# Crossbar transposes for two more units of a chunk-selected attention with a gated FFN, row copies as transfers, and an instruction order drawn anew

## The chip, the cores and the metric

One core of a Trainium2 chip runs the whole program. The metric is the time of one execution on the device in microseconds; a version's time is the median of its runs. Five engines work side by side, each through its own queue in program order: TensorE (PE, with the weight load PEld beside it), VectorE (DVE), ScalarE (ACT), GpSimd (POOL) and SyncE (SP), which here issues transfers and computes nothing.

## What is computed

The inputs q, k and v have 4 batches, 8 heads, 768 rows and 64 columns. For every query row, 6 of the 24 chunks of 32 keys are chosen by an upper bound on the score; the scores of the chosen keys at or before the row go through a softmax and weigh v. The result, 3072 rows of 512, goes through a gated feed-forward layer.

```python
k_min, k_max = k_chunks.min(axis=3), k_chunks.max(axis=3)      # 24 chunks of 32 rows
ub = sum(maximum(q * k_min, q * k_max))                        # bound for every row and chunk
ub = where(row // 32 >= chunk, ub, -1e9)
top_chunks = argsort(ub)[..., -6:]
scores = where(chosen & (row >= column), q @ k.T / 8, -1e9)
attn_out = softmax(scores) @ v
x = attn_out as 3072 x 512
out = (sigmoid(x @ w_gate) * (x @ w_val)) @ w_out              # 512 -> 1536 -> 512
```

## The kernel before

The 24 blocks of 128 rows (4 batches of 6) are put into eight units of up to three blocks. Unit 0 holds the first blocks of batches 0, 1 and 2; unit 1 three blocks of batch 0; unit 2 the last two blocks of batch 0 and, as a third, the first block of batch 3; units 3 to 7 hold the rest of batches 1, 2 and 3. The first block of a batch needs no choice of chunks and goes through a helper of its own, `first()`.

What a unit goes through:

- **Keys and queries.** They come in by `load_first`, `load_wide` (units 1 and 2) or `load_blocks` (batches 1 to 3: four transfers of 384 KB each for `k` and for `q`, named `k00_3` to `k11_3` and so on), and are turned so that the head's columns lie on partitions. `first()` and `turned()` turn on TensorE against an identity; `keys_blocks()` and `turn_queries()` turn on VectorE. The turned keys are copied by rows into `hk` (`hk0_*` and `hk1_*`, 64 partitions each), the queries into `hq`, the chunks' minima and ranges into `kcr` (`kx0`, `kx1`).
- **The choice.** `choose()` computes the bounds on TensorE (`ub`), takes the sixth largest per row on VectorE, and writes the mask, turned back, into the other 64 partitions of `hq` (the copies `hqm0_*`, `hqm1_*`), so that the score product adds it.
- **Attention.** `attend()`: score banks on TensorE (`sc`), the exponential on ScalarE (`exp`), the triangle on GpSimd (`cm`), the product with v (`pv`), and in `finish()` the division on VectorE (`rz`, `x`).
- **The turn of the result.** The attention rows `x` are turned into `xT` for the feed-forward layer. In `finish()` units below `XBAR` do it with `xps` (one TensorE transpose for each block) and a copy `xT` out of PSUM on ACT or DVE; units from `XBAR` on with one crossbar transpose on SP (`xT`, L905). `XBAR` is 4.
- **The feed-forward layer.** Units 0 to 3 each have their own: 12 pairs of `g` and `v` (four matmuls of 384 columns each), a tanh on ACT, `hg` on DVE, then `o0`, `o1`, `o2` (four matmuls of 512 columns each) for each of three blocks. Units 4 and 5, and 6 and 7, go through it as pairs, with seven products for eight (`ffn_pair`): products P1 to P7, sums of weights `Sg`, `Sv` and `So`, sums of activations `T` on DVE, copies `E` and additions `C` on ACT and DVE, `hg`, then sums S1 to S4 on POOL or DVE and the projection Q1 to Q7.

No loop sets the order of the instructions. `Plan.add` records every operation with its reads, writes, candidate engines and costs; a string `ORDER` in the file names all operations in one line of text, with the engine (`@POOL`) and the buffer slots (`:0,3`) of each, and `Plan.order()` emits them in that order, each into its engine's queue. The order was drawn by a planner that is not in the file; the costs, the transfers' times (`dma=`) and a mark `port=True` for operations that it is to keep from meeting on a shared port are what it is given. Buffers come in numbered slots, so a transfer into a slot waits for the last reader of what was there: `k_3` takes the slot of `k_2`, `q_3` that of `q_2`, the `v` blocks take six.

SP's queue holds the loads, the stores and the crossbar transposes. GpSimd's queue holds the loads of the three weights.

Of the kernel before, what the change touches and what calls it, by code (L numbers as in the profile page):

```python
# [15 lines left out]
XBAR = 4  # L16
# [103 lines left out]
g_u0_11:1,0,11 kx1_u2_3 cm_u1_0 sc_u1_0_1:4 kt_u2_3@DVE:0 v_u0_11:7 hkf1 exp_u1_0_1 kx0_u2_3 tanh_u0_9 v16_0_3  # L120
o0_u0_0:4,0 kt_u2_0:2 hg_u0_9 tanh_u0_11 hk1_u2_3@POOL hk1_u2_0 kt_u2_1:1 sc_u1_1_1:5 q2_u2 o1_u0_0 hg_u0_11
hk0_u2_1@ACT q3_u2 kx0_u2_1 exp_u1_1_1 k11_1:0 hq1_u1_0 qf1_3:2 v16_0_2 o2_u0_0 v16_0_1 hk0_u2_3@POOL pv_u1_2:6
osb_u0_0@DVE kfT_3:3 qn_u2_3:4 sc_u1_5_0:2,2 kcr_u2 qn_u2_2:2 pv_u1_1:1 kf16_3@DVE:0 qf0_3 pv_u1_0 qT_u2_3:7 out_u0_0
rz_u1_0:0 qT_u2_2:0 sc_u1_6_2:5,3 pv_u1_3 k01_1 qf_u2_2 sc_u1_7_0:4,0 exp_u1_5_0 rz_u1_1:1 o0_u0_1:3,1 vf_3:1 qm_u2_2
qf_u2_3@DVE hq0_u2_2 x_u1_0:0 exp_u1_6_2 sc_u1_7_2:0 sc_u1_4_2:2,1 x_u1_1:2 exp_u1_7_2 sc_u1_7_1:7 o1_u0_1 exp_u1_4_2
qm_u2_3 exp_u1_7_0 qm_u2_0 sc_u1_5_2:1 hq1_u2_1 sc_u1_6_0:5 cm_u1_7 exp_u1_7_1 sc_u1_5_1:0 cm_u1_5 exp_u1_5_1
sc_u1_4_0:6 ub_u2:2,4 k10_1 exp_u1_6_0 k00_1 exp_u1_5_2 xps_u1_0:7,1 exp_u1_4_0 sc_u1_6_1:0 ubn0_u2:0 sc_u1_4_1:5
qfT_3:1 xT_u1_0 exp_u1_4_1 cm_u1_4 mx0_u2:0 o2_u0_1 hk0_u2_0@ACT hq0_u2_3@POOL ubn1_u2 exp_u1_6_1 hq1_u2_3@POOL
pv_u1_5:2 qf16_3:6 mx1_u2 cm_u1_6 pv_u1_7:6 vc_3@ACT pv_u1_4 v_0_5:5 hq1_u2_0@DVE pv_u1_6 rz_u1_2:0 scf_3:7,5,0 ap1_u2
# [15 lines left out]
g_u1_10:2,3,3 tanh_u1_9 qf0_u3_3 v_u1_10:0 v_1_4:1 tanh_u1_10 hg_u1_9 qm_u3_2@POOL exp_u2_5_0 sc_u2_5_2:4
g_u1_11:5,0,5 hg_u1_10 hk1_1_0@ACT x_u2_0:1 v_u1_11:2 hg_u1_8 cm_u2_5 hq0_u3_2@ACT ub_u3:3,6 cm_u2_4 v_2_1:5
hq0_u3_0@POOL tanh_u1_11 v_1_2:3 hk1_1_3@ACT hg_u1_11 v16_1_0 o0_u1_0:0,1 ubn1_u3:0 hq1_u3_0@ACT hk0_1_1 qf0_u4_2
k01_2 xps_u2_0:7 o1_u1_0 ubn0_u3 hk0_1_0 hk0_1_3@ACT ubm1_u3 mx1_u3:0 o2_u1_0 exp_u2_5_2 ubm0_u3 ap1_u3 xT_u2_0@ACT
hq1_u3_2 o0_u1_1:1,0 osb_u1_0 qf0_u4_3 mx0_u3 sc_u2_5_1:5 out_u1_0 o1_u1_1 exp_u2_5_1 ap0_u3 hk0_1_2@ACT apt1_u3:0
q10_2:1 pv_u2_5:2 apt0_u3 pv_u2_6:6 q00_2 pv_u2_4 hqm1_u3_2@ACT hqm0_u3_0@DVE hqm0_u3_2 o2_u1_1 kx1_2_2:1 hk1_1_2  # L150
sc_u3_0_0:3,3 sc_u3_0_1:4 xps_u2_1:7 exp_u3_0_0 sc_u3_0_2:0 sc_u3_1_0:5,1 rz_u2_2:0 hqm1_u3_0 pv_u2_7 x_u2_2:2
osb_u1_1 o0_u1_2:3,1 kx1_2_1 q11_2 xT_u2_1@ACT cm_u3_0 exp_u3_0_1 sc_u3_1_1:2 exp_u3_1_0 rz_u2_3:0 kx0_2_1
sc_u3_3_0:1,0 exp_u3_0_2 sc_u3_6_1:7,2 o1_u1_2 cm_u3_1 exp_u3_1_1 x_u2_3:1 k16_2_3@ACT:5 v16_1_2 kx0_2_0 sc_u3_1_2:4
out_u1_1 k16_2_0:4 exp_u3_1_2 sc_u3_3_2:5 o2_u1_2 k16_2_1@ACT:1 kx1_2_0 xps_u2_3:0 xps_u2_2:4 xT_u2_2 xT_u2_3@ACT
# [10 lines left out]
hq1_u4_0@POOL cm_u3_5 v16_2_2 hq1_u4_2@POOL v_1_5:0 v16_1_5 cm_u3_4 hg_u2_6 mx0_u4 ap0_u4 apt0_u4:0 hqm0_u4_2
qf0_u5_1:1 tanh_u2_8 g_u2_9:3,2,13 v_u2_9:4 g_u2_10:1,3,14 tanh_u2_9 hg_u2_7 hg_u2_9 exp_u3_7_2 exp_u3_5_1 sc_u3_4_1:6
hqm0_u4_0@DVE pv_u3_6:2 tanh_u2_10 hg_u2_8 v_u2_10:7 hg_u2_10 g_u2_11:4,2,15 v_u2_11:0 exp_u3_4_1 sc_u4_2_0:7,2
sc_u4_2_3:6 exp_u4_2_3 hk0_2_1 v_2_0:2 hk1_2_1 k01_3 k00_3 k16_3_0:4 kx0_3_0 k16_3_3:0 exp_u4_2_0 cm_u4_2 v16_1_4
pv_u3_5:1 xps_u3_0:3 sc_u4_2_1:5 exp_u4_2_1 tanh_u2_11 pv_u3_7 rz_u3_3:0 x_u3_3:2 o0_u2_0:6,1 sc_u4_3_2:5,3 exp_u4_3_2
pv_u3_4 sc_u4_0_2:4,1 sc_u4_0_3:2 exp_u4_0_3 sc_u4_3_0:7 exp_u4_3_0 hg_u2_11 o1_u2_0 o2_u2_0 osb_u2_0 sc_u4_1_0:7,0  # L170
sc_u4_3_1:2 v_3_2:0 sc_u4_3_3:5 exp_u4_3_3 xT_u3_0 qf0_u6_0 qf0_u5_3 ap1_u4 qf0_u5_2 rz_u3_2:0 sc_u4_2_2:3 hk1_2_3
qf0_u5_0 cm_u4_3 v16_2_0 exp_u4_1_0 cm_u4_1 o0_u2_1:0,0 o1_u2_1 kx1_3_3:1 hk1_2_0 hq0_u5_2@POOL hq1_u5_2@POOL
qm_u5_2@ACT:0 sc_u4_1_1:7 exp_u4_3_1 qm_u5_0@ACT exp_u4_0_2 x_u3_2:1 sc_u4_1_3:1 o2_u2_1 exp_u4_1_3 kx0_3_3 kt_3_0:3
apt1_u4 kx0_3_1 kt_3_3:4 hqm1_u4_0 xps_u3_3:2 osb_u2_1 q11_3:1 k16_3_1:5 q10_3 out_u2_0 xps_u3_2:5 xT_u3_2@ACT
o0_u2_2:6,1 kx1_3_2 ub_u5:0,1 ubn1_u5:0 ubn0_u5 mx0_u5:0 kx1_3_0 ap0_u5 kt_3_1:0 sc_u4_1_2:5 hqm1_u4_2@ACT sc_u4_0_0:4
exp_u4_0_0 hq1_u5_0@POOL hq0_u5_0@POOL xT_u3_3@ACT o1_u2_2 o2_u2_2 g_u3_0:2,2,0 v_u3_0:4 exp_u4_2_2 pv_u4_2:3
# [1188 lines left out]
```

## Time and profile before

| | |
|---|---|
| median of 3 runs | 288.0 us (287.28 to 288.57) |
| the profiled execution | 286.49 us, of which the span from the first to the last instruction 284.5 us |
| mean granted TensorE clock | 0.998 |
| instructions | PE 2668, DVE 660, ACT 457, POOL 231 |
| moved by the transfers | 34.28 MB, mean 120 GB/s |
| crossbar transposes | 16, all on SP's queue |

The profile shows one execution. A busy time is a sum over an engine's instructions; a strip of 40 digits gives the busy share in tenths of 40 equal slices of the span (7.1 us each). Matmuls overlap: a single one of 384 columns shows 326 ns, while four in a row take 0.65 us, so a duration that is to be added up is read from start to start. The last 2 us of the execution's time (286.49 less 284.5) lie outside the span.

### The profile page before, as it was taken

What the parts mean: (1) busy time and instruction counts of PE and PEld (TensorE: products, weight loads), DVE (VectorE), ACT (ScalarE), POOL (GpSimd) and SP (SyncE); (2) the same over time, 40 slices, a digit from 0 to 9 for tenths busy, and PEclk for the clock granted to TensorE, in tenths of its full rate; (3) what the DMA queues carried; (4) which work ended last, traced back from release to release, by engine and by line L of the source; (5) the groups of instructions that cost most, each with busy time, mean ns of one, the idle gap of its engine ahead of it and who ended that gap; (6) DMA issues with size and microseconds to landing.
All of it is one profiled execution on the core that took longest, in us unless ns stands there. A gap on an engine that the chain in (4) does not pass through costs nothing.

```text
span 284.5 us, 7266 instructions
## 1 busy us (share of the span) xinstructions
PE 265.6 (93%) x2668; PEld 180.9 (64%) x2668; DVE 248.8 (87%) x660; ACT 209.5 (74%) x457; POOL 162.1 (57%) x231
## 2 busy tenths in 40 slices
PE   1859999799999999999999999999899999999994
PEld 1637565567764666664767756676476786765784
DVE  6569987569998998989979899999999989999972
ACT  2477579488779788668799997899899647758621
POOL 7298634246257559569776866357848700076720
PEclk9999999999999999999999999999999999999999
DMA  7999999999999999919335013030000211001005
GB/s 169 254 214 219 213 197 206 197 186 221 186 181 215 188 247 210 175 30 216 80 75 140 6 30 81 37 69 13 16 14 17 64 40 75 2 37 76 1 2 221
DMA packets 130035, 34.28 MB, mean 120 GB/s; under 512 B 118096, under 2 KB 127056, under 8 KB 130000
## 3 DMA queue, kind: packets, MB, share of 16 engines
q1 hardware_dynamic: 125248, 29.11, 48.5%
q0 software_dynamic: 4752, 4.72, 9.9%
q8 instruction: 21, 0.34, 0.5%
q14 instruction: 14, 0.11, 0.1%
HBM read 30.67 MB, written 6.29 MB: 130 GB/s over the span
## 4 chain that ended last, share of the span: by engine, by line
PE 66%; DVE 11%; DMA 9%; SPq 4%; ACT 3%; POOL 3%; issue 2%; DVEq 0%; POOLq 0%; ACTq 0%
PE sc_u L848 9%; PE o_u L968 9%; PE g_u L937 8%; PE v_u L937 8%; PE pv_u L881 5%; DMA kq_u<-in_k_dram 5%; DMA v<-in_v_dram 4%; PE suo_u6u L1195 3%; PE suo_u4u L1195 2%; PE ube_u L787 2%; PE suv_u6u L1054 2%; DVE hg_u L1084 2%; PE sug_u6u L1054 2%; DVE hgp_u L1084 2%; SPq L538 2%
## 5 line engine op out<-in xcount | busy, mean ns | idle before, releaser
L859 ACT ACTIVATE att_u<-sc_u 128x512 f16<-128x512 f32 (+3 forms) x184 | 92.1, 552 | 15.9 <-PE sc_u L848 14.4
L865 POOL TENSOR_SCALAR_AFFINE_SELECT att_u<-att_u 128x384 f16<-128x384 f16 (+1 forms) x56 | 30.7, 556 | 44.3 <-ACT att_u L859 35.5
L937 PE MATMUL g_u<-xT_u,wg 128*128 128x384 f16 x192 | 39.1, 326 | 0.1
L937 PE MATMUL v_u<-xT_u,wv 128*128 128x384 f16 x192 | 39.0, 326 | 0.1
L968 PE MATMUL o_u<-wo,hg_u 128*128 128x512 f16 x144 | 35.3, 379 | 1.0 <-DMA wo<-in_moe_w_out_dram 1.0
L949 DVE SCALAR_TENSOR_TENSOR hg_u<-gate_u,v_u 128x384 f16<-128x384 f16 x48 | 25.1, 535 | 4.3 <-PE v_u L937 2.4
L881 PEld LDWEIGHTS <-att_u 128*128 128x128 f16 x640 | 24.9, 98 | 5.5 <-issue 1.5
L881 PE MATMUL pv_u<-v,att_u 128*128 128x65 f16 x640 | 27.3, 193 | 1.1 <-POOL v L564 1.0
L945 ACT ACTIVATE gate_u<-g_u 128x384 f16<-128x384 f32 x48 | 23.3, 495 | 6.7 <-PE g_u L937 6.5
L848 PE MATMUL sc_u<-hqe,hke 128*128 128x128 f16 (+2 forms) x220 | 27.8, 243 | 0.1
L848 PE MATMUL sc_u<-hqo,hko 128*128 128x128 f16 (+2 forms) x220 | 27.3, 243 | 0.1
L937 PEld LDWEIGHTS <-wg 128*128 128x128 f16 x192 | 18.1, 98 | 10.4 <-issue 0.8
L937 PEld LDWEIGHTS <-wv 128*128 128x128 f16 x192 | 18.1, 98 | 10.5 <-DMA wv<-in_moe_w_val_dram 0.4
L968 PEld LDWEIGHTS <-hg_u 128*128 128x128 f16 x144 | 13.2, 98 | 13.7 <-DVE kcr L572 1.3
L848 PEld LDWEIGHTS <-hke 128*128 128x128 f16 x220 | 17.0, 98 | 7.3 <-issue 1.0
L848 PEld LDWEIGHTS <-hko 128*128 128x128 f16 x220 | 16.8, 98 | 6.4 <-issue 0.9
L1177 POOL TENSOR_TENSOR v<-v,hg_u 128x384 f16<-128x384 f16 x6 | 6.0, 996 | 24.1 <-PE sug_u6u L1054 22.3
L564 POOL CAST v<-v 128x512 f16<-128x512 f32 x23 | 14.8, 644 | 7.0 <-DMA v<-in_v_dram 5.8
L900 DVE TENSOR_TENSOR x_u<-pv_u,rz_u 128x384 f16<-128x384 f32 (+1 forms) x28 | 14.7, 529 | 0.6
L1054 PEld LDWEIGHTS <-Sg 128*128 128x128 f16 x96 | 9.1, 98 | 6.1 <-issue 1.4
L810 DVE MAX8 mx_u<-ubn_u 128x8 f32<-128x8 f32 (+16 forms) x152 | 12.5, 158 | 0.3
L1054 PEld LDWEIGHTS <-Sv 128*128 128x128 f16 x96 | 9.0, 98 | 5.4 <-issue 0.5
(280 smaller groups left out, 699.3 us busy)
## 6 DMA issues: line engine op xcount, KB each, us to landing
v<-in_v_dram SPq DMA_DIRECT2D x23, 256.0 KB, 4.1
k<-in_k_dram SPq DMA_DIRECT2D x12, 384.0 KB, 5.0
q<-in_q_dram SPq DMA_DIRECT2D x12, 384.0 KB, 5.0
out_dram<-osb_u SPq DMA_DIRECT2D x16, 256.0 KB, 2.6
wg<-in_moe_w_gate_dram POOLq DMA_DIRECT2D x3, 512.0 KB, 11.5
wv<-in_moe_w_val_dram POOLq DMA_DIRECT2D x3, 512.0 KB, 12.8
wo<-in_moe_w_out_dram POOLq DMA_DIRECT2D x3, 512.0 KB, 20.3
out_dram<-osb_u6u SPq DMA_DIRECT2D x5, 256.0 KB, 2.4
```

The lines of the kernel that those rows point to most:

```text
L564: plan.add(f"v16_{b}_{ib}", {POOL: pool(H * D)}, lambda e: nc.gpsimd.tensor_copy(v16[b % 2][:, ib, :, 0:D], at(t)), reads=[t], writes=[("v ...
L848: nc.tensor.matmul(at(t)[:, o:o + 128 * m], hk[b % 2][e_][:, p, 128 * jb:128 * jb + 128], hq[u.side][e_][:, p, 128 * x:128 * (x + m)], sta ...
L859: plan.add(f"exp_{u.name}_{h}_{y}", {ACT: act(n)}, lambda e, t=t, att=att, b0=b0, n=n: nc.scalar.activation(at(att)[:, b0:b0 + n], at(t), ...
L865: nc.gpsimd.affine_select(out=dv, in_=dv, compare_op=ALU.is_ge, fill=0.0, base=0, pattern=[[0, u.m], [1, 128]], channel_multiplier=-1)
L881: nc.tensor.matmul(at(pv)[:, last, x, :], at(att)[:, c:c + 128], v16[b % 2][:, jb, h, :], start=(jb == 0), stop=(jb == ib))
L900: plan.add(f"x_{u.name}_{p}", {DVE: dve(u.t)}, lambda e: nc.vector.tensor_tensor(at(x_).rearrange("p a (e d) -> p e a d", e=2), at(pv)[:, ...
L937: nc.tensor.matmul(at(t), w16[:, c, 128 * fb:128 * fb + 128], at(u.xt)[:, c, :], start=(c == 0), stop=(c == 3))
L945: plan.add(f"tanh_{u.name}_{fb}", {ACT: act(T)}, lambda e, g=g, gate=gate: nc.scalar.activation(at(gate), at(g), AF.Tanh, scale=0.5), read ...
L949: plan.add(f"hg_{u.name}_{fb}", {DVE: dve(T)}, lambda e, w_=w_, gate=gate, hg=hg: nc.vector.scalar_tensor_tensor(at(hg), at(gate), 1.0, at ...
L968: nc.tensor.matmul(at(o), hgs[c][1][1]()[:, 128 * tb:128 * tb + 128], wo16[:, fc, lo:hi], start=(c == 0), stop=(c == NFB - 1))
L1054: nc.tensor.matmul(at(t), left[i](c), right[i](c), start=first and c == 0, stop=c == 1, skip_group_check=not first)
L1195: nc.tensor.matmul(at(t), sums[what[i][0], f][1]()[:, 128 * tb:128 * tb + 128], what[i][1](f), start=first and f == 0, stop=f == half - 1, ...
```

## The change

`XBAR` goes from 4 to 2: units 2 and 3 turn their attention rows by crossbar transposes too (4 transfers each in place of 8 and 12 TensorE transposes and 8 copies out of PSUM). In `first()`, the fourth batch's block, which belongs to unit 2, does the same with its queries, keys and result: two casts to 16 bits (`qfc_3` on POOL, `kfc_3` on ACT) and two crossbar transposes take the place of eight 32-bit TensorE transposes and two copies out of PSUM, and two crossbar transposes that of four TensorE transposes and two copies. The row copies `hk` of batches 2 and 3 and `hqm` of units 4 to 7 may be plain transfers on SP; in the new order 12 of the former and 9 of the latter are. `hg` of the pairs gets the mark `port=True` unless one source is PSUM. The order is drawn anew: it is the same up to about 40 us and another after that. Crossbar transposes go from 16 to 28, and SP issues 33 transfers more in all.

The code, without the string of the order:

```diff
-XBAR = 4
+XBAR = 2
...
@@ -353,6 +353,8 @@
             nc.scalar.copy(o, i)
         elif e == DVE:
             nc.vector.tensor_copy(o, i)
+        elif e == SP:
+            nc.sync.dma_start(o, i)
         else:
             nc.gpsimd.tensor_copy(o, i)
 
@@ -593,6 +595,14 @@
         cols = slice(128 * x, 128 * x + 128)
         half = {}
         for n in "kq":
+            if u.i >= XBAR:
+                flat = Buf("np", f"{n}fc_{b}", [128, H * D], F16)
+                plan.add(f"{n}fc_{b}", {POOL: pool(H * D), DVE: dve(H * D, 2), ACT: act(H * D, False)}, lambda e, n=n, flat=flat: copy(
+                    e, at(flat), at(raw[n]).rearrange("s h d -> s (h d)")), reads=[(raw[n], 0), (raw[n], 1)], writes=[flat], port=True, prio=next_())
+                half[n] = Buf("np", f"{n}f16_{b}", [128, NP, 128], F16)
+                plan.add(f"{n}f16_{b}", {SP: (60, 60)}, lambda e, h=half[n], flat=flat: nc.sync.dma_start_transpose(out=at(h), in_=at(flat)),
+                         reads=[flat], writes=[half[n]], prio=next_(), dma=(1200, 256))
+                continue
             t = ps(f"{n}fT_{b}", "pr", [128, NP, 128])
 
             def turn(e, t=t, n=n):
@@ -659,6 +669,12 @@
             plan.add(f"xf_{b}_{e_}", {DVE: dve(256)}, lambda e, pv=pv, rz=rz, x_=x_: nc.vector.tensor_tensor(
                 at(x_), at(pv)[:, :, 0:D], at(rz).unsqueeze(2).to_broadcast([128, NP, D]), ALU.mult),
                 reads=[pv, rz], writes=[x_], prio=next_())
+            if u.i >= XBAR:
+                op = plan.add(f"xTf_{b}_{e_}", {SP: (60, 60)}, lambda e, x_=x_, e_=e_: nc.sync.dma_start_transpose(
+                    out=at(u.xt)[:, 2 * e_:2 * e_ + 2, cols], in_=at(x_).rearrange("s p d -> s (p d)")),
+                    reads=[x_], writes=[(u.xt, c, x) for c in (2 * e_, 2 * e_ + 1)], prio=next_(), dma=(1200, 256))
+                plan.hold(op, u.xt) if u.xt not in op.bufs else None
+                continue
             t = ps(f"xpsf_{b}_{e_}", "pr", [128, 2, 128], F16)
 
             def turn(e, t=t, x_=x_):
@@ -738,7 +754,7 @@
             plan.add(f"kt_{b}_{p}", {DVE: dve(S)}, lambda e, k16=k16, kt=kt: nc.vector.transpose(
                 at(kt), at(k16).rearrange("p c d -> p (c d)")), reads=[k16], writes=[kt], prio=next_())
             for e_ in range(2):
-                plan.add(f"hk{e_}_{b}_{p}", {POOL: pool(S), DVE: dve(S, 4, 64), ACT: act(S, False, 64)},
+                plan.add(f"hk{e_}_{b}_{p}", {POOL: pool(S), DVE: dve(S, 4, 64), ACT: act(S, False, 64), **({SP: (60, 60)} if b > 1 else {})},
                          lambda e, p=p, e_=e_, kt=kt: copy(e, hk[par][e_][ROWS[e_], p], at(kt)[ROWS[e_]]),
                          reads=[kt], writes=[("hk", par, jb, e_, p) for jb in blocks], port=True, prio=next_())
         ranges(par, f"{b}", kx, slice(0, NC), blocks, next_)
@@ -822,7 +838,8 @@
                 at(apt)[:, e_], ap[u.side][:, e_, 0:u.nb].rearrange("p c d -> p (c d)")),
                 reads=[("ap", u.side, e_)], writes=[(apt, e_)], prio=next_())
             for p in range(0, NP, 2):
-                plan.add(f"hqm{e_}_{u.name}_{p}", {POOL: pool(2 * u.n), DVE: dve(2 * u.n, 4, 64), ACT: act(2 * u.n, False, 64)},
+                plan.add(f"hqm{e_}_{u.name}_{p}", {POOL: pool(2 * u.n), DVE: dve(2 * u.n, 4, 64), ACT: act(2 * u.n, False, 64),
+                                                   **({SP: (60, 60)} if u.i > 3 else {})},
                          lambda e, p=p, e_=e_: copy(
                              e, hq[u.side][e_][MASK[e_], p:p + 2, u.s0:u.t],
                              at(apt)[32 * p:32 * p + 64, e_, :].unsqueeze(1).to_broadcast([64, 2, u.n])),
@@ -1083,7 +1100,7 @@
                         plan.add(f"hg_{tag}_{x}_{fb}", {DVE: dve(T)},
                                  lambda e, src=src, g=g, o=o: nc.vector.scalar_tensor_tensor(
                                      o(), at(g), 1.0, at(src), ALU.add, ALU.mult), reads=[g, src], writes=[okey],
-                                 prio=next_(EV))
+                                 port=c != 2, prio=next_(EV))
 
                 op = mul(1, u_, True)
                 for b in (q_, r_):
```

Of the order, one place that the prediction speaks of: the loads of batch 3's keys and the crossbar transposes of unit 3 on SP. Between these words stand those of other engines.

```
... k01_3 v_3_5 hk0_2_1@SP out_u1_0 k10_3 xT_u3_1 k00_3 k11_3 v_2_4 hk1_2_0@SP v_2_0 xT_u3_0 xT_u3_3 xT_u3_2 ... g_u3_0 ...
```

More of the change, by code (lines that the diff above doesn't have):

```diff
@@ L120 @@
[L120 to L129, printed above, removed]
@@ L145 @@
[L145 to L154, printed above, removed]
@@ L165 @@
[L165 to L174, printed above, removed]
@@ new lines @@
+g_u0_10:4,3,10 tanh_u0_10 v_u0_10:6 kT_u2_3:7 hq1_u1_1@POOL hq1_u1_0@POOL v16_0_3 cm_u1_3 hk0_u2_0 g_u0_11:4,1,11
+v_u0_11:2 tanh_u0_11 hg_u0_11 kx0_u2_2 hq0_u2_0@POOL hk1_u2_1@POOL sc_u1_0_1:0 o0_u0_0:4,0 o1_u0_0 hg_u0_9 hg_u0_10
+o2_u0_0 exp_u1_0_1 kx1_u2_3 v16_0_2 qm_u2_0@POOL osb_u0_0 kx0_u2_1 kx1_u2_2 kx1_u2_1 kx0_u2_3 k01_1 o0_u0_1:1,1
+o1_u0_1 v16_0_1 pv_u1_2:4 sc_u1_6_1:5,2 hk1_u2_2@ACT kt_u2_3@DVE:0 hqm1_u1_0@DVE hk0_u2_3@ACT sc_u1_6_2:7 cm_u1_0
+pv_u1_0:6 exp_u1_6_1 exp_u1_6_2 pv_u1_1 rz_u1_0:0 x_u1_0:1 k11_1 sc_u1_7_1:3,3 k00_1 sc_u1_5_0:5,1 exp_u1_5_0 pv_u1_3
@@ new lines @@
+xT_u3_3 ap1_u4 qf0_u6_0 qf0_u6_1 apt1_u4 hqm1_u4_0 pv_u3_5 rz_u3_2:0 x_u3_2:1 xT_u3_2 kx1_3_2:1 exp_u4_3_1 ub_u5:0,6
+ubn0_u5:0 hqm1_u4_2@ACT sc_u4_1_0:4,1 exp_u4_1_0 sc_u4_1_2:1 exp_u4_1_2 exp_u4_3_3 sc_u4_2_0:7 exp_u4_2_0
+hq1_u5_0@POOL o1_u2_1 o2_u2_1 q01_3:1 q10_3 cm_u4_3 hk0_2_0 k16_3_1:1 sc_u4_2_2:7 exp_u4_2_2 q00_3 osb_u2_1 out_u2_1
+kx1_3_0 kx0_3_2 kx0_3_0 kx0_3_1 sc_u4_4_2:2,3 exp_u4_4_2 exp_u4_2_1 mx0_u5:0 hq0_u5_0@ACT sc_u4_4_1:1 v16_2_0
+exp_u4_4_1 o0_u2_2:4,1 o1_u2_2 o2_u2_2 g_u3_0:5,2,4 cm_u4_2 v_u3_0:2 tanh_u3_0 g_u3_1:1,3,8 k16_3_3@ACT:6 v_u3_1:5
```

290 lines of the change are left out of this document (155 added, 135 removed).

## The prediction

> **What bounds the kernel now.** I read the page's engine totals and strips first, to see which engine is full where.
>
> ```profile
> PE 265.6 (93%) x2668; PEld 180.9 (64%) x2668; DVE 248.8 (87%) x660; ACT 209.5 (74%) x457; POOL 162.1 (57%) x231
> ...
> PE   1859999799999999999999999999899999999994
> ...
> DVE  6569987569998998989979899999999989999972
> ...
> DMA  7999999999999999919335013030000211001005
> ```
>
> TensorE is the fullest engine and has holes only at the start, around slice 7, and at the end. The transfers fill their engines up to slice 17 (121 us), which is where most of the new transfers go. VectorE is at nine tenths nearly everywhere. Next the busy times by stage, cut at 60, 120, 176 (just ahead of the first product of the pair of units 4 and 5) and 268 (where the last projections begin).
>
> ```profile
> 30.00:60.00 30.00, 27.71 (x270) 17.36 (x269) 21.65 (x81) 20.87 (x52) 11.51 (x23) 1.00 1.11 200
> 60.00:120.00 60.00, 59.90 (x644) 39.29 (x643) 56.53 (x170) 49.05 (x104) 36.50 (x58) 1.00 1.09 202
> 120.00:176.00 56.00, 56.00 (x717) 37.76 (x715) 52.02 (x166) 45.61 (x94) 42.85 (x56) 1.00 0.41 85
> 176.00:268.00 92.00, 89.63 (x796) 60.73 (x794) 88.27 (x177) 73.83 (x172) 45.98 (x55) 1.00 0.12 37
> ```
>
> The first column after the stretch is its length, then PE, PEld, DVE, ACT and POOL busy; the last three are the granted clock, the transfers' share and GB/s. From 60 to 176 us TensorE idles 0.1 of 116 us: each matmul taken out there is time, and each late transfer too. From 176 to 268 TensorE idles 2.4 us and VectorE 3.7: two bounds side by side. Last, what TensorE waited for.
>
> ```profile
> PE qfT L600 <- POOL hke L357: 5.8, 1, 5.8
> ...
> PE pv_u L881 <- POOL v L564: 1.0, 1, 1.0
> PE o_u L968 <- DMA wo<-in_moe_w_out_dram: 1.0, 1, 1.0
> ```
>
> The 5.8 us is the start. The two waits of 1.0 us stand at 50 and 52 us, behind 40 us, from where the order is new.
>
> **The change part by part.** *The turns leave TensorE.* Two places of the timeline show what one costs from start to start.
>
> ```profile
> 52.51 0.63 PE L600 MATMUL kfT<-ident,kf 128*128 128x128 f32 x4
> 52.98 0.39 PE L848 MATMUL sc_u<-hqo,hko 128*128 128x128 f16 x4
> ...
> 95.81 0.28 PE L914 MATMUL xps_u<-ident,x_u 128*128 128x128 f16 x2
> 95.92 0.49 PE L848 MATMUL sc_u<-hqe,hke 128*128 128x256 f16 x5
> ```
>
> Four 32-bit turns take 0.47 us until the next matmul starts, two 16-bit ones 0.11. Eight of the former go (0.94) and 24 of the latter (8 for unit 2, 12 for unit 3, 4 for the fourth batch's first block: 1.32). Sum **-2.3 us**, all ahead of 176 us, where TensorE does not idle. The 12 copies out of PSUM that go with them, less the two new casts, are ACT's and DVE's, off the path there.
>
> *The order moves matmuls.* Counted in the two lists, three more output thirds (`o`), six more score banks, one `pv` and five pair products stand ahead of 176 us, and three projection steps `Q` move from behind 268 us to ahead of it.
>
> ```profile
> 99.25 0.86 PE o_u L968 x4
> 102.93 0.65 PE g_u L937 x4
> 233.25 0.66 PE suo_u4u L1195 x6
> ```
>
> At 0.86 for a third, some 0.2 for a score bank (four times the 0.055 above), 0.3 for a `pv` and 0.33 for a product (two matmuls of the second row's size), that is 2.6 + 1.2 + 0.3 + 1.6 = 5.7 us out of the stage from 176 on; three `Q` at 0.66 bring 2.0 into it and take 2.0 from the end. This moves work and saves none; it says which engine has to carry the pair stage.
>
> *The wait for v at 52 us.* In the new order `o0_u0_1` and `o1_u0_1` (1.7 us) stand between `o2_u0_0`, which waits for `wo`, and `pv_u1_2`, which waited 1.0 us for the cast of v. The cast itself gets one more GpSimd operation ahead of it, but no later load. I take **-1.0**; at worst it stays, 0. The wait for `wo` stays.
>
> *The pair stage.* VectorE decides with TensorE here. These are its groups from 176 us on, with busy time and mean.
>
> ```profile
> L1084 DVE SCALAR_TENSOR_TENSOR hgp_u<-gate_u4u,c3v_u4u 128x384 f16<-128x384 f16 x6 | 4.8, 801 | 0.0
> L1084 DVE SCALAR_TENSOR_TENSOR hgp_u<-gate_u4u,c1v_u4u 128x384 f16<-128x384 f16 x6 | 4.5, 748 | 0.0
> L1084 DVE SCALAR_TENSOR_TENSOR hg_u<-gate_u6u,c0v_u6u 128x384 f16<-128x384 f16 x6 | 4.4, 735 | 0.1
> L1084 DVE SCALAR_TENSOR_TENSOR hgp_u<-gate_u6u,c1v_u6u 128x384 f16<-128x384 f16 x6 | 4.1, 684 | 0.3
> L1084 DVE SCALAR_TENSOR_TENSOR hg_u<-gate_u4u,c0v_u4u 128x384 f16<-128x384 f16 x6 | 4.1, 684 | 0.2
> L1084 DVE SCALAR_TENSOR_TENSOR hgp_u<-gate_u6u,c3v_u6u 128x384 f16<-128x384 f16 x6 | 3.9, 645 | 0.4 <-ACT gate_u6u L1079 0.2
> ...
> L1084 DVE SCALAR_TENSOR_TENSOR hg_u<-gate_u4u,suv_u4u 128x384 f16<-128x384 f16 x6 | 3.3, 544 | 0.0
> ...
> L821 DVE STREAM_TRANSPOSE apt_u<-ap 128x384 f16<-128x384 f16 x2 | 1.1, 567 | 0.0
> L1019 DVE TENSOR_TENSOR T_u4u<-xT_u,T_u4u 128x768 f16<-128x768 f16 x2 | 1.1, 545 | 0.0
> ```
>
> The 36 `hg` whose sources both lie in SBUF take 25.8 us; at the 0.544 of those with one source in PSUM they would take 19.6. So 6.2 us of VectorE's time are a slowdown, and the sums S on GpSimd run in the same stretches (35 of 48, about 0.92 us each by the row below). The new order puts 30 on GpSimd and, through the mark on `hg`, is drawn to keep the two apart. The Trainium skill, SBUF — State Buffer, section "Who interferes with whom", says that a VectorE operation with two SBUF inputs and a reading GpSimd operation share one port pair as an exclusive lock, the loser blocked for the whole instruction. By that rule all of the 6.2 us go with an order that keeps them apart, and TensorE alone would set the stage; the trace agrees that only the two-SBUF form is stretched.
>
> ```profile
> L1177 POOL TENSOR_TENSOR hgp_u<-hg_u,hgp_u x8: 902/916/1224, 201.8 to 272.3; 128x384 f16<-128x384 f16 x8
> ...
> L1177 DVE TENSOR_TENSOR hgp_u<-hg_u,hgp_u x4: 344/348/1060, 229.7 to 273.4; 128x384 f16<-128x384 f16 x4
> ```
>
> VectorE's own list from 176 to 268 gains eight sums S (0.35 each) and one each of `hg` and a copy (0.55), and loses two turns `apt`, three `T`, two additions, one `x` (all about 0.55) and one weight sum (about 1): 3.9 in, 5.4 out, **-1.5**. TensorE's list there is 5.7 - 2.0 = 3.7 shorter. So the 92 us shrink by 1.5 if no slowdown goes and VectorE sets the stage, and by at most 3.7 + 2.4 = 6.1 if TensorE sets it without idling. A planned order meets the chip only roughly, so I let something under half of the 6.2 go, 2.7, and take **-4.2**.
>
> *Sum of the stages.* Up to 176: -2.3 + 5.7 - 1.0 = +2.4. From 176 to 268: -4.2. Behind: -2.0. Together -3.8.
>
> *New waits.* The nearest rows for a turn by crossbar, and for the loads that now stand beside it:
>
> ```profile
> v<-in_v_dram SPq DMA_DIRECT2D x23, 256.0 KB, 4.1
> k<-in_k_dram SPq DMA_DIRECT2D x12, 384.0 KB, 5.0
> ...
> xT_u<-x_u SPq DMA_TRANSPOSE x8, 3.1
> ...
> L905 SPq DMA_TRANSPOSE xT_u<-x_u x8: 1187/1201/2322, 140.9 to 174.7; - x8
> ...
> 211.00:214.00 3.00, 3.00 (x36) 2.10 (x35) 3.00 (x7) 3.00 (x8) 1.32 (x2) 1.00 0.15 33
> ```
>
> A turn holds SP's queue for 1.2 to 2.3 us and lands after some 3; of the transfer engines it takes 0.15 of 3.0 us, 0.45 us (that window holds one and nothing else). In the lists the matmuls between a new transfer's place and its first use take 13 us for `qf16_3`, 6 for the last `xT` of units 2 and 3, and for the row copies 5 to 30, bar `hk0_2_1` (3), `hqm0_u5_2` (2) and `hk1_2_3` (0, though SP's queue runs ahead of that place). Most are hidden; the last three are bare, and if SP runs level with the list each costs up to its landing, 2 to 4 us less its lead. Row copies leave GpSimd and ACT and free nothing on the path. I take **+0.8** for the whole, two waits of the size of those of today; the bottom is 0, since TensorE idled 0.1 us there, the top the first rival. The Trainium skill, DMA: Bandwidth & Descriptors, section "Anatomy of one DMA — SWDGE (gpsimd) path", puts a fixed cost near 2 us on a transfer, most of it the receipt of the last byte; for SP's queue the trace has that too (0.45 of work, 3.1 to land).
>
> Net: -3.8 + 0.8 = **-3.0**. The profiled execution took 286.5 (a span of 284.5 and 2.0 around it), 1.5 below the median of 288.0. Against that median: **285.0 us**.
>
> **The rivals.** *The transfers of unit 3 come too late (slower).* On SP, `xT_u3_2` stands behind `k01_3` and what follows it: four loads of 384 KB, three of 256, a store of 256, two row copies and four turns of 96, 3.2 MB, 15.9 us at the 202 GB/s of the row from 60 to 120, against 9 us of matmuls from that place to `g_u3_0`. Counted from `q00_2` it is 5.3 MB or 26 us against 22. SP then has to run 4 us ahead of the list; if it doesn't, because a wait for a slot (`v_2_2` and `v_1_4` wait for casts that wait for scores) holds everything behind it, `g_u3_0` waits those 4 us and a landing, 5 to 6 in all, and TensorE, in order, does nothing else meanwhile. That is 285.0 + 5.5 = 290.5. For it: SP's queue is one, the transfers' share is 1.09. Against it: between 60 and 125 us SP waited some 20 us for others (eleven rows, the first two and the last below), time in which it could have issued. The Trainium skill, DMA: Bandwidth & Descriptors, section "Queues, rings and completion order", says descriptors start in ring order, which is this rival's rule; the rows show loads landing after 4 to 5 us there, so it holds so far only for a few us.
>
> ```profile
> SPq L548 <- DVE kcr L572: 4.9, 2, 3.7
> SPq L979 <- ACT osb_u L977: 3.6, 2, 2.7
> ...
> SPq L979 <- ACT gate_u L945: 0.3, 1, 0.3
> ```
>
> *VectorE keeps the pair stage (no change).* If the slowdown of `hg` stays, the stage gives 1.5 in place of 4.2: 285.0 + 2.7 = 287.7. For it: VectorE 88.3 of 92 us. Against it: TensorE's waits for VectorE there are few.
>
> *The mark works whole (much faster).* The stage gives 6.1 and no new wait shows: 285.0 - 1.9 - 0.8 = 282.3.
>
> **How the numbers follow.** The forecast with its own spread has a chance of 0.43, the whole gain 0.14, VectorE keeping the stage 0.19, the late transfers 0.24. The range goes from 281.5, just under the best case, to 290.0, which takes in half of the late transfers' cases; 0.15 is left out. About 0.5% (1.4 us) is what a measurement of this kernel can tell from no change: faster means under 286.6, slower over 289.4. The forecast and the whole gain give 0.57 faster, VectorE 0.19 the same, the late transfers 0.24 slower.
>
> **What would show it.** Right: 12 `xps` matmuls left of 32 and 24 turns in `first()` of 32 in 32 bits; `pv_u` waiting for the v cast no more; TensorE idle by under 1 us from 60 to 176 us; the 36 `hg` near 22 us in place of 25.8. Wrong: `g_u` of unit 3 or `sc_u` of units 4 and 5 waiting on a DMA by more than 2 us, or VectorE at over 97% from 176 on with `hg` as slow as now.

## The result, and the profile after

The changed kernel takes **305.45 us** (median of 4, 303.96 to 307.59) against 287.64 for the kernel before on the same chip: 1.0624 times as long, interval 1.0579 to 1.0669. (Ratios are taken from the means of the runs and differ a little from those of the medians.) Forecast were 285.0 us and a range of 281.5 to 290.0. The profiled execution took 305.57 us, with a span of 303.6.

The page of the changed kernel: TensorE's row, three strips, and the queue of SP's transfers (packets, MB, and the time its packets took as a share of 16 engines' span).

```profile
PE 270.3 (89%) x2636; PEld 181.8 (60%) x2636; DVE 244.4 (80%) x656; ACT 201.5 (66%) x434; POOL 154.5 (51%) x227
...
PE   1859999978989796799849999999999989999995
...
PEclk9977999997999999599997999999999999999999
DMA  7999999999999899999999246420022010201105
...
q1 hardware_dynamic: 131984, 32.22, 66.5%
```

The holes in the PE strip lie in slices 8 to 20 (counted from 0; a slice is 7.6 us here), where there were none, and the transfers stay full for 22 slices (167 us) in place of 17 (121 us). The transfers of the turns and row copies add 5% of packets (131,984 against 125,248); the time of the queue's packets went from 48.5% of a span of 284.5 to 66.5% of 303.6, that is by 46%. The same by stage, then the landings (KB each, median us from issue to landing):

```profile
60.00:120.00 60.00, 52.18 (x493) 32.31 (x490) 42.62 (x107) 37.95 (x77) 30.41 (x47) 0.97 1.21 151
120.00:176.00 56.00, 47.90 (x526) 30.45 (x534) 41.47 (x131) 34.59 (x71) 29.98 (x40) 0.91 1.09 149
```

```profile
v<-in_v_dram SPq DMA_DIRECT2D x23, 256.0 KB, 5.3
k<-in_k_dram SPq DMA_DIRECT2D x12, 384.0 KB, 7.4
q<-in_q_dram SPq DMA_DIRECT2D x12, 384.0 KB, 7.2
```

From 60 to 120 us the transfer engines are fuller than before (1.21 against 1.09) and move less (151 GB/s against 202). So it is not more work that fills them; the same work takes longer. A load of `k` lands after 7.4 us in place of 5.0. TensorE then waits, through engines that stand still themselves: ahead of the wait of 3.9 us VectorE stood 5.5 us for a load of `q` (until 121 us), ahead of the one of 3.7 ACT stood 4.5 us for a store that still read its `osb` slot (until 158 us). What VectorE stood for ahead of the 2.5 us, at 69 us, the profile does not name.

```profile
PE v_u L954 <- DVE x_u L917: 5.1, 2, 3.9
PE sc_u L865 <- ACT gate_u L962: 3.7, 1, 3.7
PE sc_u L865 <- DVE hg_u L966: 2.9, 2, 2.5
```

The packet records of the traces say which transfers became slow. Behind 50 us both kernels move 73,728 packets of 128 B, the `load_blocks` transfers: a mean of 12.9 ns each before and **20.8 ns** after. The fourth column of the table below has it for each kernel.

### The profile page after: what moved, and what is told of

Its sections match the earlier page's. It is cut to its first block, busy times and chain, and to the rows that moved or that the text cites. A ratio compares the mean times of both kernels' runs of the same rounds, so it can differ in the third digit from the quotient of the medians.

```text
span 303.6 us, 7252 instructions
## 1 busy us (share of the span) xinstructions
PE 270.3 (89%) x2636; PEld 181.8 (60%) x2636; DVE 244.4 (80%) x656; ACT 201.5 (66%) x434; POOL 154.5 (51%) x227
## 3 DMA queue, kind: packets, MB, share of 16 engines
q1 hardware_dynamic: 131984, 32.22, 66.5%
## 4 chain that ended last, share of the span: by engine, by line
PE 56%; DVE 15%; DMA 15%; SPq 6%; ACT 3%; issue 3%; DVEq 0%; ACTq 0%
PE sc_u L865 9%; PE v_u L954 6%; DMA q<-in_q_dram 6%; PE g_u L954 6%; PE o_u L985 4%; PE pv_u L898 4%; DMA k<-in_k_dram 3%; PE suo_u6u L1212 3%; SPq L550 2%; PE sug_u6u L1071 2%; PE suv_u6u L1071 2%; PE sug_u4u L1071 2%; DMA out_dram<-osb_u 2%; PE ube_u L803 2%; SPq L529 2%
## 5 line engine op out<-in xcount | busy, mean ns | idle before, releaser
L954 PE MATMUL v_u<-xT_u,wv 128*128 128x384 f16 x192 | 41.6, 342 | 5.1 <-DVE x_u L917 5.1
L954 PE MATMUL g_u<-xT_u,wg 128*128 128x384 f16 x192 | 41.1, 338 | 0.2 <-DVE hg_u L966 0.2
L865 PE MATMUL sc_u<-hqo,hko 128*128 128x128 f16 (+2 forms) x220 | 29.4, 248 | 4.9 <-ACT gate_u L962 3.7
L865 PE MATMUL sc_u<-hqe,hke 128*128 128x128 f16 (+2 forms) x220 | 27.0, 247 | 5.1 <-DVE hg_u L966 2.9
L954 PEld LDWEIGHTS <-wv 128*128 128x128 f16 x192 | 19.0, 102 | 17.8 <-DVE x_u L917 4.2
L985 PEld LDWEIGHTS <-hg_u 128*128 128x128 f16 x144 | 13.5, 98 | 13.7 <-issue 0.5
L590 POOL TENSOR_SCALAR qm_u<-qf_u 128x768 f32<-128x768 f32 (+3 forms) x11 | 17.3, 1581 | 6.5 <-DVE qf_u L770 6.1
L770 DVE STREAM_TRANSPOSE qf_u<-q 128x384 f32<-128x384 f32 (+2 forms) x28 | 11.4, 437 | 8.7 <-DMA q<-in_q_dram 8.7
L574 DVE TRANSPOSE_TENSOR_REDUCE kx<-k 128x24 f32<-128x768 f32 x12 | 11.3, 953 | 5.1 <-issue 2.7
L1194 POOL TENSOR_TENSOR v<-hgp_u 128x384 f16<-128x384 f16 x5 | 5.0, 998 | 19.9 <-DVE hgp_u L1101 17.0
## 6 DMA issues: line engine op xcount, KB each, us to landing
wo<-in_moe_w_out_dram POOLq DMA_DIRECT2D x3, 512.0 KB, 19.6
```

What stands on the lines that cost most here:

```text
L590: (nc.vector if e == DVE else nc.gpsimd).tensor_scalar_max(o, i, 0.0)
L865: nc.tensor.matmul(at(t)[:, o:o + 128 * m], hk[b % 2][e_][:, p, 128 * jb:128 * jb + 128], hq[u.side][e_][:, p, 128 * x:128 * (x + m)], sta ...
L954: nc.tensor.matmul(at(t), w16[:, c, 128 * fb:128 * fb + 128], at(u.xt)[:, c, :], start=(c == 0), stop=(c == 3))
L985: nc.tensor.matmul(at(o), hgs[c][1][1]()[:, 128 * tb:128 * tb + 128], wo16[:, fc, lo:hi], start=(c == 0), stop=(c == NFB - 1))
```

## The experiments

**Two theories.** *A, the addresses.* The pool `head` stands ahead of all other pools and holds one slot, `kx0`. A slot is as large as its largest tile. Before, slot 0 holds `kx_f` (64 B per partition), `kx_u2` (128) and `kx_1` (4 x 24 numbers of 4 B, 384), so 384 B. The new order says `kx1_u2_0:1` and `kx1_1_3:1` where the old one says `kx1_u2_2:0` and `kx1_1_1:0`; slot 0 is left with `kx_f`, 64 B. Every later tile therefore moves down by 320 B: `k_1` from 53,760 (a multiple of 128) to 53,440, which is 64 past one. A 128 B packet no longer begins and ends on multiples of 128 B, it lies across one. *B, the queue.* In the new order block loads follow each other directly, and crossbar turns stand among them; that slows the packets.

The first four runs tell them apart. Each adds one unused tile and nothing else.

```diff
+    head.tile([128, 80], F32, tag="pad", name="pad")      # 320 B; 16, 48 and 32 columns for 64, 192 and 128 B
     pools = {"ps": banks, "kx0": head, "big": land, "v": land, "osb": land}
```

> The changed kernel with one unused tile of 320 B per partition in the pool `head`, so that every later tile stands 320 B higher, where the kernel before has it (k_1 at 53760 in place of 53440, a multiple of 128 again); order, instructions and transfers are untouched. Theory A (the addresses: slot kx0 shrank from 384 B to 64 B, all tiles moved by 320 B and the 128 B packets of the k and q block loads now end in the middle of a 128 B line): these packets take 13 ns again and not 20 on average, the DMA engines come to rest near 130 us and not 167 us, and the time is 282 to 290 us. Theory B (the queue: block loads issued back to back, with crossbar turns among them, slow each other): packets stay at 20 ns and the time at 304 to 307 us.

> The kernel before with one unused tile of 192 B per partition in the pool `head`: every later tile stands 192 B higher, at the same remainder of 128, 256 and 512 B as in the changed kernel; nothing else differs. Theory A (addresses): the 128 B packets go from 13 ns to 19 to 25 ns, the loads between 50 and 140 us take half as long again, and the time rises to 295 to 306 us. Theory B (queue): 287 to 289 us and 13 ns as before.

> The changed kernel with 64 B in place of 320 B: all tiles at a multiple of 256 B but not of 512 B. Theory A in the form that 128 B is the boundary that counts: within 1 us of the run with 320 B, packets at 13 ns. Theory A in the form that 512 B counts: 304 to 307 us still. Theory B: 304 to 307 us.

> The kernel before with 128 B more in `head`: all tiles at an odd multiple of 128 B. Theory A with the boundary at 128 B: 287 to 289 us, packets at 13 ns. Theory A with the boundary at 256 B or 512 B: 295 to 306 us. Theory B: 287 to 289 us.

Two more move the k and q block tiles alone, by 64 B within their slots: off the boundary in the kernel before, back onto it in the unpadded changed kernel.

```diff
-        t = Buf("big", f"{n}_{b}", [128, NP, NC, CH])
+        t = Buf("big", f"{n}_{b}", [128, NP * NC * CH + 32])
 ...
+            if b.name[:2] in ("k_", "q_"):
+                b.tile = b.tile[:, 16:16 + NP * NC * CH].rearrange("s (p c d) -> s p c d", p=NP, c=NC)
```

> The kernel before in which the k and q block tiles alone begin 64 B into their slots (the slots are 128 B larger, so every other tile stays on a multiple of 128 B). Theory A1 (only the destination of the 128 B packets counts): packets at 19 to 22 ns and 303 to 307 us, as with the whole of the memory moved. Theory A2 (the other transfers and the engines' accesses suffer too and make up a good part): 288 to 298 us.

> The changed kernel without padding, all tiles 64 B past a multiple of 128 B as they fell, in which the k and q block tiles alone begin 64 B into their slots and so stand on a multiple of 128 B. Theory A1: 128 B packets at 13 ns and 288 to 290 us, as with all tiles moved back. Theory A2: 293 to 303 us.

| kernel | block tiles, past 128 B | other landing tiles | mean of a 128 B packet | median us | ratio to before, same chip |
|---|---|---|---|---|---|
| before | 0 | 0 | 12.9 ns | 287.64 | |
| changed | 64 | 64 | 20.8 ns | 305.45 | 1.0624 (1.0579 to 1.0669) |
| changed, 320 B | 0 | 0 | 12.9 ns | 289.00 | 1.0083 (1.0053 to 1.0112) |
| changed, 64 B | 0 | 0 | 13.0 ns | 288.29 | 1.0066 (1.0036 to 1.0096) |
| before, 192 B | 64 | 64 | 19.7 ns | 306.33 | 1.0673 (1.0630 to 1.0717) |
| before, 128 B | 0 | 0 | 13.2 ns | 288.66 | 1.0068 (1.0030 to 1.0107) |
| before, blocks off | 64 | 0 | 20.9 ns | 305.28 | 1.0644 (1.0583 to 1.0706) |
| changed, blocks on | 0 | 64 | 13.2 ns | 290.82 | 1.0108 (1.0047 to 1.0168) |

The ratio is to the kernel before as it ran beside each: 287.64 us on the chip of the changed kernel, 286.52 and 286.38 us on those of the other rows.

Theory A holds, theory B falls. 320 unused bytes, with the order as it is, bring the changed kernel from 6.2% over the kernel before to 0.8%; 192 put 6.7% onto the kernel before, whose order has fewer loads back to back (9 of the 24 block loads follow the one ahead without a gap, 12 in the padded changed kernel) and whose crossbar turns all stand behind them (the first at 140.9 us). Two forecasts were missed narrowly, 306.33 us where theory A said at most 306, and 290.82 where A1 said at most 290; and the padded kernel's transfers stay full until about 150 us, not 130. A shift by an odd multiple of 128 B is nearly harmless, so 128 B is the boundary that counts. Moving the block tiles alone does nearly all of it, both ways (A1). Here is the padded kernel in the views shown above:

```profile
PE 262.6 (92%) x2636; PEld 178.3 (62%) x2636; DVE 245.6 (86%) x656; ACT 200.5 (70%) x434; POOL 155.0 (54%) x227
...
DMA  7999999999999599999993574300021100201105
...
q1 hardware_dynamic: 131984, 32.22, 54.8%
```

```profile
60.00:120.00 60.00, 56.92 (x604) 36.43 (x603) 52.17 (x133) 43.34 (x90) 38.48 (x57) 1.00 0.99 187
120.00:176.00 56.00, 54.76 (x694) 36.71 (x692) 50.25 (x189) 45.59 (x93) 35.42 (x47) 1.00 0.79 149
```

```profile
v<-in_v_dram SPq DMA_DIRECT2D x23, 256.0 KB, 4.6
k<-in_k_dram SPq DMA_DIRECT2D x12, 384.0 KB, 4.9
q<-in_q_dram SPq DMA_DIRECT2D x12, 384.0 KB, 5.0
```

The same instructions, the same packets: 54.8% in place of 66.5%, 4.9 us in place of 7.4. For the two kernels in which only the blocks moved, first off, then on:

```profile
k<-in_k_dram SPq DMA_DIRECT2D x12, 384.0 KB, 7.4
q<-in_q_dram SPq DMA_DIRECT2D x12, 384.0 KB, 7.6
```

```profile
k<-in_k_dram SPq DMA_DIRECT2D x12, 384.0 KB, 5.5
q<-in_q_dram SPq DMA_DIRECT2D x12, 384.0 KB, 5.4
```

The loss has two halves. The spans differ by 17.7 us (303.6 and 285.9). TensorE's idle time is 33.3 us against 23.3, which is 10.0; its busy time for the same 2636 matmuls is 270.3 against 262.6, which is 7.7. The second half is mostly the granted clock: 0.97 and 0.91 in the two stages above, 1.00 in both with the padding. In the trace's clock records it is at half for 13.7 us in these stages, in three stretches (from 70.4, 121.6 and 159.2 us), which is worth at most half of that, 6.8 of the 7.7 us. The Trainium skill, "TensorE: Matmul & The Clock Gate", Part 1, says that a gate lets through half the pulses after an idle window of about 3.4 us. The last two stretches begin in or at the end of the waits of 3.9 and 3.7 us, which fits; the first follows a wait of 2.5 us alone, which is shorter than that.

**What is left.** With the addresses out of the way the kernel is still 0.7 to 0.8% over the kernel before, where a gain was forecast. (The kernel before, moved by 128 B, is over it by as much, so the time alone does not show that the change costs this; the waits do.) From 60 to 176 us, where TensorE waited for nothing before, these are the padded kernel's longest waits:

```profile
PE v_u L956 <- DVE x_u L919: 1.7, 1, 1.7
...
PE sc_u L867 <- ACT gate_u L964: 1.2, 1, 1.2
PE sc_u L867 <- DVE x_u L919: 1.2, 1, 1.2
```

The timeline shows what is behind each: VectorE at 94 us, VectorE and TensorE at 112 us, ACT at 142 us.

```profile
93.91 0.42 DVE L919 TENSOR_TENSOR x_u<-pv_u,rz_u 128x256 f16<-128x256 f32 x1 [1.49 <-DMA xT_u<-xf]
...
111.72 1.16 DVE L772 STREAM_TRANSPOSE qf_u<-q 128x128 f32<-128x128 f32 x4 [2.85 <-DMA q<-in_q_dram]
...
113.06 0.52 DVE L919 TENSOR_TENSOR x_u<-pv_u,rz_u 128x384 f16<-128x384 f32 x1
```

```profile
113.65 0.82 PE L956 MATMUL v_u<-xT_u,wv 128*128 128x384 f16 x4 [1.72 <-DVE x_u L919]
```

```profile
142.13 0.60 ACT L996 ACTIVATE osb_u<-o_u 128x512 f32<-128x512 f32 x1 [1.53 <-DMA out_dram<-osb_u]
```

Three times an engine's queue stands still for a transfer: `x_u2_2` for its slot, from which a crossbar turn still reads; the turns of the fourth batch's queries for the load `q11_2`, with `x_u3_1` behind them, for which TensorE waits; `osb_u2_2` for its slot, from which a store still reads. Two theories on that: *L*, the turns by crossbar and the full queue of SP make these transfers late; *O*, the redrawn order does. Four runs take parts out or put them in alone.

```diff
 # turns back on TensorE, order after:           -qfc_3:2 ... qf16_3:4     +qfT_3:0 ... qf16_3@ACT:4
                                                  -xT_u2_1                  +xps_u2_1:3 ... xT_u2_1@ACT     (twelve in all)
 # turns by crossbar, order before:               -xps_u2_0:7 ... xT_u2_0@ACT   +xT_u2_0                    (twelve, or eight)
 # row copies off SP, order after:                -hk0_2_1@SP               +hk0_2_1@POOL                   (21 in all)
```

> The changed kernel with the 320 B of padding, and the twelve turns that the change gave to the crossbar (units two and three, the fourth batch's first block) back on TensorE, each four to fourteen places behind where its transfer stood; the redrawn order and the row copies on SP stay. TensorE's own work grows by 2.2 us against the padded kernel (289.0 us). Theory L (SP's queue is full from 60 to 145 us, the turns by crossbar hold it and the transfer engines, and the three waits of TensorE at 94, 112 and 142 us, 4.3 us in all, come from that): most of these waits go, 286 to 288 us. Theory O (the waits belong to the redrawn order of loads, the turns are free): they stay, 290.5 to 291.5 us.

> The kernel before, with its own order and addresses, and all twelve turns by crossbar: each stands in SP's queue where TensorE's turn stood, the copy out of PSUM is gone, the two casts are on GpSimd and ACT. TensorE's work falls by 2.2 us. If the turns are free (theory O): 284 to 285 us. Theory L: the loads of the second to fourth batch land later by the turns' hold of SP's queue and new waits of 2 to 5 us give the gain back: 286 to 289 us.

> As the run with all twelve turns by crossbar in the order of the kernel before, but unit two's four turns stay on TensorE: only the fourth batch's first block (four turns) and unit three (four turns, from about 120 us, where the transfer engines have room in this order) go to the crossbar. TensorE's work falls by 1.8 us. Theory L: little is given back, 284.5 to 286 us, and below the run with all twelve. Theory O: 284.5 to 285.5 us, 0.4 us above the run with all twelve.

> The changed kernel with the 320 B of padding and the 21 row copies back on the engines that have them in the kernel before (15 on GpSimd, four on VectorE, two on ACT). If the row copies in SP's queue are what costs (rival): 286 to 287.5 us. Theory L and theory O: only four of them stand ahead of 145 us, where SP is full, so within 1 us of 289.0 us, or slower by what GpSimd (15 copies of some 0.8 us) takes from VectorE through their common port.

| kernel | median us | ratio to before, same chip |
|---|---|---|
| changed, 320 B, turns on TensorE | 293.65 | 1.0255 (1.0212 to 1.0298) |
| before, twelve turns by crossbar | 301.43 | 1.0526 (1.0483 to 1.0569) |
| before, eight turns by crossbar | 296.06 | 1.0338 (1.0293 to 1.0384) |
| changed, 320 B, row copies off SP | 301.77 | 1.0542 (1.0504 to 1.0581) |

The kernel before took 285.89 us on their chip. All four are slower than either theory said (the fourth left room for slower, but through VectorE's port), and the time of none of them separates L from O: each edit by hand in a drawn order cost more than the part is worth. The waits say more. Turns on TensorE: all three waits are gone, the one for the `q_2` loads too, which is L's direction. But new waits come from where I put the turns and their copies, 3.2 us between 84 and 93 us; TensorE comes to the first `g` of unit 2 3.6 us later than in the padded kernel (103.3 and 99.7 us) and SP issues the first of the `q_2` loads behind it only 0.9 us later (100.4 and 99.4), so that the transfers had more time. So this run does not decide it. The first of the new waits, and VectorE's turns of the `q_2` queries, ahead of which it no longer stands still:

```profile
PE ube_u L807 <- ACT xT_u L357: 1.5, 1, 1.5
```

```profile
113.81 1.14 DVE L774 STREAM_TRANSPOSE qf_u<-q 128x128 f32<-128x128 f32 x4
```

Twelve turns by crossbar in the old order: TensorE waits for two of them for 9.3 us, since that order leaves them no time to land, and its clock is at half for 6.8 us behind each of the two waits.

```profile
PE g_u L954 <- DMA xT_u<-x_u: 5.2, 2, 4.9
PE scf L647 <- DMA qf<-qfc: 4.4, 1, 4.4
```

Row copies off SP: some 13 us more than with them (1.0542 and 1.0083). TensorE waits 9.7 us for GpSimd, mostly at 157 and 176 us, where a copy and the triangles of the scores stand behind other copies in its queue.

```profile
PE pv_u L900 <- POOL att_u L884: 7.3, 4, 4.9
...
PE sc_u L867 <- POOL hko L361: 2.4, 1, 2.4
```

The last two runs go at the three waits themselves, and then at two more.

```diff
-x_u2_2:2 ... x_u2_3:0
+x_u2_2:1 ... x_u2_3:2
-q11_2 qf1_u4_2 exp_u3_0_1 qf1_u4_3 qf1_u4_1 qf0_u5_3:1 ... qf1_u4_0 x_u3_1:0 tanh_u2_6 hg_u2_6
+q11_2 exp_u3_0_1 ... x_u3_1:0 tanh_u2_6 hg_u2_6 qf1_u4_2 qf1_u4_3 qf1_u4_1 qf1_u4_0 qf0_u5_3:1
-osb_u2_2 ... tanh_u3_3
+... tanh_u3_3 osb_u2_2
 # and for the five edits:
-sc_u4_0_0:4,2        S3_u4u5_1@POOL S3_u4u5_2@POOL S3_u4u5_5@POOL
+sc_u4_0_0:3,2        S3_u4u5_1 S3_u4u5_2 S3_u4u5_5
```

> The changed kernel with the 320 B of padding and three edits for TensorE's waits at 94, 112 and 142 us: x of unit two takes the slots 1 and 2 in place of 2 and 0 (their transfers have landed by then); the five turns of the fourth batch's queries on VectorE that wait for the last q_2 load stand behind x_u3_1 and hg_u2_6 and not ahead of them; osb_u2_2 on ACT stands behind tanh_u3_3. Theory L (these waits are what is left of the loss, each through a queue that stands still for a late transfer): 1.2, 1.8 and 1.3 us go, less what comes next, so 285 to 287 us against 289.0. Rival (TensorE runs into the next late transfer, the stage is as long as its transfers): within 1 us of 289.0.

> The padded changed kernel with the three edits, and two more: sc_u4_0_0 takes the free PSUM slot 3 in place of 4, so that TensorE no longer waits there for osb_u2_2 (1.4 us at 141 us); the sums S3_u4u5_1, _2 and _5 go from GpSimd to VectorE, since GpSimd runs them at 226 to 230 us ahead of their place in the list while four operations of VectorE beside them take 0.95 to 1.26 us in place of 0.35 to 0.63, and TensorE waits 2.1 us for those sums at 228 to 232 us. If both waits were on the path: 283.5 to 285.5 us against 287.2 with three edits and 286.4 before. Rival (VectorE, full from here on, loses with three more sums what it wins, and the next late transfer takes the first): 286.5 to 287.5 us.

Three edits: 287.19 us against 286.38, ratio 1.0021 (0.9993 to 1.0050). Five: 285.48 us against 286.05, ratio 0.9983 (0.9951 to 1.0015). Of 4.1 us of waits the three edits bring 1.8 (0.6%), a little less than the 2 us that theory L said at least; at 141 us `osb_u2_2` still comes late:

```profile
PE sc_u L867 <- ACT osb_u L996: 1.4, 1, 1.4
```

With five edits the longest wait near 141 us is 0.8, and of some 2 us of waits between 223 and 233 us, at the sums, 1.5 come back at a later sum:

```profile
PE suo_u4u L1214 <- DVE hgp_u L1196: 1.5, 1, 1.5
```

So the waits were on the path. Whether the turns and SP's queue (L) or the redrawn order (O) make these transfers late stays open: the three edits move the operations that wait and the slots, not the transfers. The step from three to five edits is within the noise (the intervals overlap). The changed kernel, put right, stands level with the kernel before: a tie, no gain that these runs can tell.

## Why the prediction was wrong

**The step that is missing.** My sum has no term for where tiles lie. I read the two lists for engines, places and sizes of transfers, and passed over the slot numbers. The section on new waits took the landings of the kernel before (4.1 us for `v`, 5.0 for `k`) as given; they became 5.3 and 7.4. By the ratios that is 5.4 of the 6.2 percentage points, about 15.5 of the 17.8 us. What I did name as a sign of error came in the form of waits for VectorE and ACT that were themselves waiting for transfers. In the unpadded trace the first rival, late transfers, looks confirmed; the padding shows that the transfers were late because they were slow.

**The other steps**, on the padded kernel. Its marks and those of the kernel before on TensorE, padded first: the first product of units 4 and 5, and the last projections.

```profile
183.48 0.49 PE L1073 MATMUL sug_u4u<-xT_u,wg 128*128 128x384 f16 x2
...
271.30 0.82 PE L1214 MATMUL suo_u6u<-wo,hg_u 128*128 128x256 f16 x6
```

```profile
176.48 0.48 PE L1054 MATMUL srg_u4u<-T_u4u,Sg 128*128 128x384 f16 x2 [0.22 <-DVE T_u4u L1019]
...
267.68 0.82 PE L1195 MATMUL suo_u6u<-wo,hg_u 128*128 128x256 f16 x6
```

| stage | forecast | measured |
|---|---|---|
| up to the first product | +2.4, and +0.8 of new waits | 183.5 - 176.5 = +7.0 |
| the pair stage | -4.2 | (271.3 - 183.5) - (267.7 - 176.5) = -3.4 |
| behind | -2.0 | (285.9 - 271.3) - (284.5 - 267.7) = -2.2 |
| span | -3.0 | +1.4 |

About 1 of the +7.0 stands ahead of the change: of the matmuls that are the same in both orders the 200th starts at 36.7 us before and at 37.9 in the padded execution, the last, the 235th, at 41.3 and 42.1; the padded execution's clock was at half from 18 to 25 us. The other 6 are 2.8 over the forecast's 3.2, and the new waits (below) are 3.3 over the 0.8.

- *The turns leave TensorE:* right in kind. 32 matmuls fewer (2668 and 2636), as counted. In the run with the turns back, they take 2.2 us from start to start (two of them stand ahead of a wait and are counted like the others); the forecast was 2.3.
- *The wait for v at 52 us:* right. It was 1.0 us and is 0.3 at most in the changed kernel.
- *The pair stage:* right in mechanism and nearly in size. The 36 `hg` with two sources in SBUF add up to 23.1 us. That is the 2.7 us that I let go out of 6.2, though the sign I named was "near 22"; the 2.7 was a guess, and that it came out is luck. The mechanism shows in the run with five edits: with three sums gone from GpSimd, two sums of VectorE that had run beside them take 0.36 and 0.35 us in place of 0.95 and 1.06, and the mean of the first row below falls from 797 to 678 ns, while the other rows stay within 2.

```profile
L1103 DVE SCALAR_TENSOR_TENSOR hgp_u<-gate_u4u,c3v_u4u 128x384 f16<-128x384 f16 x6 | 4.8, 797 | 0.0
L1103 DVE SCALAR_TENSOR_TENSOR hg_u<-gate_u4u,c0v_u4u 128x384 f16<-128x384 f16 x6 | 4.0, 661 | 0.0
L1103 DVE SCALAR_TENSOR_TENSOR hg_u<-gate_u6u,c0v_u6u 128x384 f16<-128x384 f16 x6 | 3.8, 640 | 0.1
L1103 DVE SCALAR_TENSOR_TENSOR hgp_u<-gate_u6u,c3v_u6u 128x384 f16<-128x384 f16 x6 | 3.7, 609 | 0.1
L1103 DVE SCALAR_TENSOR_TENSOR hgp_u<-gate_u6u,c1v_u6u 128x384 f16<-128x384 f16 x6 | 3.4, 585 | 0.0
L1103 DVE SCALAR_TENSOR_TENSOR hgp_u<-gate_u4u,c1v_u4u 128x384 f16<-128x384 f16 x6 | 3.4, 563 | 0.0
```

The first row again, with five edits:

```profile
L1103 DVE SCALAR_TENSOR_TENSOR hgp_u<-gate_u4u,c3v_u4u 128x384 f16<-128x384 f16 x6 | 4.1, 678 | 0.0
```

- *New waits:* the second failed term, +0.8 where the padded kernel has 4.1 (1.7 + 1.2 + 1.2); TensorE idles 4.3 us from 60 to 176 us, where the sign I named was under 1. I priced a late transfer by its direct reader on TensorE and looked at the leads of the new transfers alone. The three that cost were a slot not yet free and a load that stands directly ahead of its first use, each read by VectorE or ACT, with something for TensorE behind it in that queue. I had marked `hk0_2_1`, `hqm0_u5_2` and `hk1_2_3` as bare; none of them shows among the waits.
- *Row copies "free nothing on the path":* wrong for the new order, which takes some 13 us more when they are put back by hand. There TensorE waits for what stands behind them on GpSimd.
- *The first rival* named the mechanism (SP's queue late, an in-order engine standing still) and a price of 290.5 that is near the padded 289.0, but at `g_u3_0`, which did not wait; that the price is near is chance. The second (VectorE keeps the stage) fell; the third's price was not reached.

## What to carry to other kernels

When an order or a slot assignment is drawn anew, compare the tiles' addresses too: a slot that shrinks in a pool at the front moves everything behind it, and the cost appears in transfers that nobody touched. A rise of the transfer engines' busy share with a fall of GB/s says "the same packets take longer", not "more transfers"; pad the front by the difference before anything else is explained. And price a late transfer through every engine whose queue it holds, slots that a transfer still reads included.

## What the runs showed of the hardware

- A transfer in 128 B packets to 32 partitions pays half as much again and more when its destination starts 64 B past a multiple of 128 B: 12.9 to 20.8 ns a packet. The 12 loads of 384 KB that follow the one ahead without a gap take, at the median, 2.2 us from first to last packet with the padding and 3.3 us without it, about 180 and 120 GB/s. Only loads of this shape were tried. Packets of 256 B hardly change (19.5 ns with the padding, 19.6 with the blocks alone on the boundary and the `v` tiles off it). The Trainium skill, "DMA: Bandwidth & Descriptors", section "How a descriptor splits into AXI transactions", says that a transaction starts at a multiple of 256 B. It speaks of reads, and these runs move where the packets are written. Applied to writes, every second 128 B packet at an offset of 64 B would become two transactions, and at 0 or 128 B none. The order of the runs agrees; the 256 B packets, which would be two as well, do not.
- The slowdown is not even. In the changed kernel a misaligned load that follows a gap mostly starts with its packets at 13 ns and slows to a mean of 20 to 29 ns after a third to five sixths of its 3072 packets, with single packets over 50 ns; of the 12 that follow directly, most are slow from their first packets. On the boundary 95% take 12 to 14 ns. What sets the slowdown off was not tried.
- A transfer counts as landed when the last of its 16 parts is in. Of the turn for which VectorE waits at 94 us, 15 parts had landed at 92.4 and the last at 93.8; a 16 KB instruction fetch of 0.96 us began at 91.8. That these belong together was not tested.
